# Moving the q pooling, the transposes and the last norms to other places in a kernel's fixed instruction order

## Chip, cores, metric

One core of a Trainium2 chip. The metric is the device time of one execution in microseconds (us), median of several runs. A profile of one execution has a span 1.7 to 2.3 us shorter than the time of the same run; where I compare stretches I use profiles, where I compare kernels I use timed runs. All runs here were in the fast state. Engines: PE (TensorE matmul), PEld (its weight loads), DVE (VectorE), ACT (ScalarE), POOL (GpSimd, which from slot 1 on only issues transfers).

## The reference

Attention on q averaged over pairs of positions (8 batches, 8 heads, 1152 positions, 64 wide), then a gated linear unit whose gate is a causal convolution of five taps over positions.

```python
q_pool = q.reshape(B, H, S // 2, 2, D).mean(axis=3)
scores = scale * np.matmul(q_pool, k.transpose(0, 1, 3, 2))
attn = softmax(scores)                       # over the last axis
x = np.matmul(attn, v)                       # then heads side by side: (B, S/2, 512)
gate_pre[:, s] = sum over k of conv_w[k] * x[:, s - 4 + k]
out = (sigmoid(gate_pre) * (x @ w_val)) @ w_out
```

The kernel uses that the scores are small: it replaces the softmax by its first order, so each head needs only sums and a Gram matrix of k and v, and it checks a bound on the norms at the end (the "norms" and "stat" below feed that check; an exact path exists and is not taken).

## The kernel before

The instruction order of every engine is fixed by the order in the program. (Slot 8 in the trace: while the transposes waited for 0.73 us, the value tile behind them did not start.) Sixteen slots handle two pairs of heads each, a = 2m and b = 2m + 1. Even and odd slots interleave different pieces of the second layer. These are the pieces that matter:

```python
def pool_q(n):                       # DVE: average over position pairs, as a sum
    qv = loaded.pop(n).rearrange("p h (u e d) -> p h u e d", u=U, e=2)
    nc.vector.tensor_tensor(out=qpv, in0=qv[:, :, :, 0, :], in1=qv[:, :, :, 1, :], op=ALU.add)

def transposes(n):                   # PE: 6 transposes of the pooled q; ACT copies them to SBUF
    qt_ps = ps_t.tile([128, Sq], BF16, name="qt_ps", tag="ts")      # one buffer, shared with "sm"
    ...

def sums(n): ...                     # PE: 18 matmuls into "sm" (buffer "ts")
def grams(n): ...                    # PE: 18 matmuls into g
def rows(m): ...                     # DVE: needs sm; rank1(m) on PE needs rows
def norms(m, g): ...                 # PE: 10 tiny matmuls over the squares of slot m
def stat(m, g): ...                  # DVE: copies norms out; ACT's xevac needs it
def squares(m, g): ...               # ACT
def xhat(n, at): ...                 # PE into PSUM buffer b<at>;  xevac(n): ACT
def conv(n, at): ...                 # PE into b<at>: two of the five taps
def tap(n, i): ...                   # DVE: the other three; tap 0 reads conv's PSUM
def gate(n): ...                     # ACT: sigmoid of what the taps have summed
def val(b, ft, at): ...              # PE, 8 matmuls into b<at>
def gval(b, ft, vps): ...            # DVE: gate * val, reads that PSUM buffer
def outs(...): ...                   # PE, 4 matmuls per column c into PSUM
def warm(m, at=0): ...               # PE: m matmuls on idle data, whose result nobody reads
```

The slots, cut to the lines that move (`pb` is pair b of the slot before, `moe` is true from slot 2 on):

```python
            # ---- even slot, after sums, grams, taps of pb, rank1, mevac ----
            gate(pb)
            gval(bt, 2, val(bt, 2, 0))
            norms(m - 1, g)
            stat(m, g)
            xhat(a, 1)
            xhat(b, 2)
            xevac(a)
            xevac(b)
            pool_q(a + 2)
            transposes(a + 2)
            if moe:
                v3 = val(bt, 3, 0)
                pool_q(b + 2)
                gval(bt, 3, v3)
            squares(m, g)
            conv(a, 1)
            conv(b, 2)
            tap(a, 0)
            ...                          # (slot 0 pools b + 2 here)
            tap(a, 1)
            tap(a, 2)
            outs(y, 512 * e, 2, ops, [0])
            transposes(b + 2)
            tap(b, 0)
            outs(y, 512 * e, 2, ops, [1])
            ...
            # ---- odd slot ----
            ...                          # outs, norms, stat, xhat, xevac
            pool_q(a + 2)
            outs(...)
            conv(a, 1)
            conv(b, 2)
            tap(a, 0)
            transposes(a + 2)
            pool_q(b + 2)
            gate(pb)
            tap(a, 1)
            tap(a, 2)
            gval(bt, 0, val(bt, 0, 0))
            transposes(b + 2)
            gate(a)
            gval(bt, 1, val(bt, 1, 1))
            tap(b, 0)
            squares(m, g)
            ...
    # ---- after the last slot ----
    norms(NSLOT - 1, g, start=True)
    gval(bt, 2, val(bt, 2, 0))
    gval(bt, 3, val(bt, 3, 2))
    stat(NSLOT, g)
```

All loads are issued by POOL in the order q, k, v of pair after pair, up to seven pairs ahead.

Of the kernel before, what the change touches and what calls it, by code (L numbers as in the profile page):

```python
# [54 lines left out]
def first_order(ctx, tc, q, k, v, moe_w_val, moe_conv_w, moe_w_out, out, flag):  # L55
# [9 lines left out]
    NSLOT = NPAIR // 2  # L65
# [23 lines left out]
    def big(name, i):  # L89
        return ps_b.tile([128, 2, 512], FP32, name=name, tag=f"b{i}")  # L90
# [98 lines left out]
    def pool_q(n):  # L189
        qp = work.tile([QP, U, 2, D], BF16, name="qp", tag="qp", bufs=3)  # L190
        qpv = qp.rearrange("p u h d -> p h u d")
        if n == 0:
            for h in range(2):
                qv = q0[h].rearrange("p (u e d) -> p u e d", u=U, e=2)
                nc.vector.tensor_tensor(out=qpv[:, h], in0=qv[:, :, 0, :], in1=qv[:, :, 1, :], op=ALU.add)
        else:
            qv = loaded.pop(n).rearrange("p h (u e d) -> p h u e d", u=U, e=2)
            nc.vector.tensor_tensor(out=qpv, in0=qv[:, :, :, 0, :], in1=qv[:, :, :, 1, :], op=ALU.add)  # L198
        qps[n] = qp

    def transposes(n, at=None):
        m, i = divmod(n, 2)
        qp = qps.pop(n)
        qt_ps = (ps_t if at is None else ps_b).tile([128, Sq], BF16, name="qt_ps", tag="ts" if at is None else f"b{at}")
        qtv = qt_ps.rearrange("c (u p) -> c u p", u=U)
        for u in range(U):
            nc.tensor.transpose(out=qtv[:, u, :], in_=qp[:, u].rearrange("p h d -> p (h d)"),  # L207
                                identity=ident[0:QP, 0:QP])
        nc.scalar.copy(out=mq2[m % 2][:, i, 2 * D:].rearrange("c (p u) -> c p u", u=U),  # L209
                       in_=qt_ps.rearrange("c (u p) -> c p u", u=U))  # L210
# [38 lines left out]
    def norms(m, g, start=False):  # L249
        sq = sqs.pop(m)  # L250
        for i in range(2):
            for j in range(5):
                c = 258 + 10 * i + 2 * j
                nc.tensor.matmul(out=g[:, c:c + 2], lhsT=sq[:, i, 128 * j:128 * j + 128], rhs=halves_bf,  # L254
                                 start=start and i == 0 and j == 0, stop=True, skip_group_check=True)

    def stat(m, g):
        a, z = (0 if m < NSLOT else 2), (22 if m else 2)
        nc.vector.tensor_copy(out=stats[:, m, a:z], in_=g[:, 256 + a:256 + z])  # L259
# [7 lines left out]
    def squares(m, g):  # L267
        sq = work.tile([128, 2, D + Sq], BF16, name="sq", tag="sq")
        nc.scalar.activation(out=sq[:, :, 0:D], in_=g[:, 0:256].rearrange("p (i c) -> p i c", i=2)[:, :, D:2 * D],
                             func=AF.Square, scale=C0)  # L270
        nc.scalar.activation(out=sq[:, :, D:], in_=mq2[m % 2][:, :, 2 * D:], func=AF.Square)  # L271
        sqs[m] = sq
# [62 lines left out]
    def val(b, ft, at):  # L335
        vps = big("vps", at)
        for fi in range(NFT):
            x = xs[(b * NP + fi) % NX]
            for half in range(2):
                c0 = PAD + half * HALF  # L340
                nc.tensor.matmul(out=vps[:, half, 0:HALF], lhsT=wval_sb[:, fi, ft * 128:(ft + 1) * 128],  # L341
                                 rhs=x[:, c0:c0 + HALF], start=(fi == 0), stop=(fi == NFT - 1))
        return vps

    def gval(b, ft, vps):
        y, e = divmod(b, 2)
        if e == 0:
            gvs[y, ft] = gate_pool.tile([128, 2 * Sq], BF16, name="gv", tag=f"gv{ft}", bufs=1)
        nc.vector.tensor_tensor(out=gvs[y, ft][:, e * Sq:(e + 1) * Sq].rearrange("p (c n) -> p c n", c=2),  # L349
                                in0=vps[:, :, 0:HALF],  # L350
                                in1=gates.pop(b * NP + ft).rearrange("p (c n) -> p c n", c=2), op=ALU.mult)
# [59 lines left out]
    def warm(m, at=0):  # L411
        wps = big("wps", at)
        for _ in range(m):
            nc.tensor.matmul(out=wps[:, 0, :], lhsT=idle[:, 0:128], rhs=idle, start=True, stop=True,  # L414
                             skip_group_check=True)
# [13 lines left out]
    for m in range(NSLOT):  # L429
        a, b = 2 * m, 2 * m + 1  # L430
        pb = b - 2
        odd = m % 2
        if m == 0:
            sums(a)
            grams(a)
            transposes(b, 1)
            setup_conv()
            sums(b)
            rows(m)
            grams(b)  # L440
        else:
            sums(a)
            sums(b)
            rows(m)
            grams(a)
            grams(b)
            tap(pb, 1)
            tap(pb, 2)
        rank1(m)
        g = gs.pop(m)  # L450
        mevac(m, g)
        if not odd:

            bt = m // 2 - 1
            y, e = divmod(bt, 2)
            moe = bt >= 0
# [3 lines that stand above are left out]
            else:  # L460
                warm(3)
            if m:
# [4 lines that stand above are left out]
            xevac(a)  # L467
            xevac(b)
            pool_q(a + 2)
            transposes(a + 2)  # L470
            if moe:
                v3 = val(bt, 3, 0)
                pool_q(b + 2)
                gval(bt, 3, v3)
            else:
                warm(3)
            squares(m, g)
            conv(a, 1)
            conv(b, 2)
            tap(a, 0)  # L480
            if not moe:
                pool_q(b + 2)
            tap(a, 1)
            tap(a, 2)
            if moe:
                ops = big("ops", 0)
                outs(y, 512 * e, 2, ops, [0])
            else:
                warm(2)
# [4 lines that stand above are left out]
                oevac(y, 512 * e, 2, ops)  # L494
            else:
                warm(2)
            gate(a)
        else:

            bt = (m - 1) // 2  # L500
            y, e = divmod(bt - 1, 2)
            moe = bt > 0
            if moe:
                if e:
                    ops = big("ops", 0)
                    outs(y, 1024, 1, ops)
                    oevac(y, 1024, 1, ops)
                else:
                    ops = big("ops", 0)
                    outs(y, 256, 2, ops, [0])  # L510
            else:
                warm(3)
# [5 lines that stand above are left out]
            xevac(b)  # L518
            if m + 1 < NSLOT:
                pool_q(a + 2)  # L520
            if moe:
                if e:
                    ops = big("ops", 0)
                outs(y, 256 + 512 * e, 2, ops, [0, 1] if e else [1])
                oevac(y, 256 + 512 * e, 2, ops)
            else:
                warm(3)
            conv(a, 1)
            conv(b, 2, full=m + 1 == NSLOT)
            tap(a, 0)  # L530
            if m + 1 < NSLOT:
                transposes(a + 2)
                if m > 1:
                    pool_q(b + 2)
            gate(pb)
            tap(a, 1)
            tap(a, 2)
            if m + 1 == NSLOT:
                gate(b)
            gval(bt, 0, val(bt, 0, 0))  # L540
            if 1 < m < NSLOT - 1:
# [3 lines that stand above are left out]
            if m + 1 < NSLOT:  # L545
                tap(b, 0)
            squares(m, g)
            if m == 1:
                warm(12)
                pool_q(b + 2)  # L550
                transposes(b + 2)
        while nload < min(NPAIR, a + NKV + 1):
            load_pair(nload)
            nload += 1
        if nload == NPAIR:
            while held:
                store(*held.pop(0), nc.gpsimd)


    g = ps_g.tile([128, 512], FP32, name="g", tag="g")  # L560
    norms(NSLOT - 1, g, start=True)
    gval(bt, 2, val(bt, 2, 0))
    gval(bt, 3, val(bt, 3, 2))
    stat(NSLOT, g)
    bound_reduce()
    y, e = divmod(bt, 2)
# [166 lines left out]
```

## Time and profile before

| | before |
|---|---|
| timed, median of 3 runs | 184.79 us (183.93 to 185.87) |
| span of the profile | 182.4 us |
| PE / DVE / ACT busy | 158.2 / 126.0 / 110.9 us |
| even slot 8, 10 (start to start) | 9.51, 9.74 us |
| odd slot 9, 11 | 9.38, 8.65 us |
| PE idle before the first transposes of an even slot, 2 to 14 | 0.73 us |

How to read the views: a line of the page or of the groups gives an engine's busy time; the timeline gives start and length of each stretch of like instructions, and in brackets how long the engine stood idle before and what ended it; the chain of waits is followed back from the last instruction. PE's reported ends are modelled (in slot 8 a value tile is reported as 1.15 us, and the next group starts 0.99 us after the tile's start), so I take the distance from one start to the next start for PE. (The windows in the prediction are cut at 119.50 and 128.20, where the sums of slots 11 and 12 begin at 119.52 and 128.17; hence its 9.72 and 8.70 for what is 9.74 and 8.65 from start to start.) The lines on which the reading rests are in the prediction below.

### The profile page before, as it was taken

Reading aid. Unit: us, or ns where it says so; the run is one execution under the profiler, and the core shown is the slowest. Engines: PE = TensorE matmul, PEld = TensorE weight load, DVE = VectorE, ACT = ScalarE, POOL = GpSimd, SP = SyncE. Lnnn points to the kernel's source line nnn. Section 1 sums busy time; section 2 is a strip of 40 time slices with the busy share of each in tenths; the row PEclk is TensorE's granted clock in tenths of the full one; section 3 lists DMA queues with packets and bytes.
Section 4 is the critical chain, followed back from the end, with each engine's and each line's share of the span. In section 5 each row is a group of like instructions: output and inputs, shape, how many; then the busy total and the mean of one; then the engine's idle time right before and its main releaser. Section 6 shows DMA issues by size and latency. Waiting matters only on the chain.

```text
span 182.4 us, 5370 instructions
## 1 busy us (share of the span) xinstructions
PE 158.2 (87%) x2277; PEld 111.5 (61%) x2277; DVE 126.0 (69%) x236; ACT 110.9 (61%) x183; POOL 77.3 (42%) x122
## 2 busy tenths in 40 slices
PE   7558898889998999899989999899989998997910
PEld 2146475566776667667776777577857676765400
DVE  3315678378699767978797859786978597955540
ACT  2122865347696777675967685868676878574120
POOL 7954414554544444444545444453543334410000
PEclk9957999999999999999999999999999999999985
DMA  5999999999999999999999999999999999994070
GB/s 191 275 208 210 204 206 207 207 207 207 207 206 208 208 207 207 208 206 209 205 207 208 206 207 207 206 207 207 207 207 207 222 383 414 417 390 199 0 282 20
DMA packets 27864, 40.11 MB, mean 220 GB/s; under 512 B 1909, under 2 KB 24757, under 8 KB 27834
## 3 DMA queue, kind: packets, MB, share of 16 engines
q0 software_dynamic: 26624, 36.61, 101.5%
q1 hardware_dynamic: 938, 2.50, 4.0%
q10 hardware_dynamic: 272, 0.59, 0.9%
q8 instruction: 20, 0.33, 0.7%
q14 instruction: 10, 0.08, 0.1%
HBM read 58.73 MB, written 9.44 MB: 374 GB/s over the span
## 4 chain that ended last, share of the span: by engine, by line
PE 57%; DVE 20%; DMA 13%; issue 4%; ACT 1%; POOL 1%; DVEq 0%; POOLq 0%
PE ops L357 18%; DMA qn<-in_q_dram 13%; PE vps L341 10%; DVE acc L318 6%; PE cps L303 6%; PE sm L219 6%; DVE acc L313 5%; PE g L229 5%; PE xh L280 4%; DVE qp L198 3%; PE qt_ps L207 3%; DVE gv L349 3%; PE g L254 2%; PE g L243 2%; PE wps L414 2%
## 5 line engine op out<-in xcount | busy, mean ns | idle before, releaser
L318 DVE SCALAR_TENSOR_TENSOR acc<-x,convw_sb,acc 128x576 f32<-128x576 bf16 x62 | 50.6, 815 | 1.4
L341 PE MATMUL vps<-x,wval_sb 128*128 128x288 bf16 x256 | 36.4, 286 | 0.0
L357 PE MATMUL ops<-wout_sb,gv 128*128 128x512 bf16 x144 | 36.0, 379 | 0.0
L313 DVE SCALAR_TENSOR_TENSOR acc<-x,convw_sb,cps 128x576 f32<-128x576 bf16 x31 | 25.1, 808 | 13.7 <-PE cps L303 13.7
L100 POOL DMA_DIRECT2D kv<-in_k_dram x31 | 22.2, 717 | 27.6 <-DMA kv<-in_v_dram 10.9
L99 POOL DMA_DIRECT2D qn<-in_q_dram x31 | 20.0, 645 | 29.6 <-DMA kv<-in_k_dram 11.4
L209 ACT COPY mq<-qt_ps 128x576 bf16<-128x576 bf16 x32 | 20.5, 639 | 19.7 <-PE qt_ps L207 19.0
L349 DVE TENSOR_TENSOR gv<-vps,gate 128x576 bf16<-128x576 f32 x32 | 23.5, 754 | 9.9 <-ACT mq L209 7.2
L341 PEld LDWEIGHTS <-wval_sb 128*128 128x128 bf16 x256 | 23.3, 97 | 5.8
L102 POOL DMA_DIRECT2D kv<-in_v_dram x31 | 22.2, 715 | 10.1 <-DMA qn<-in_q_dram 8.1
L287 ACT ACTIVATE x<-xh,stats 128x576 bf16<-128x576 f32 x32 | 22.0, 737 | 7.1 <-DVE stats L259 6.5
L325 ACT ACTIVATE gate<-acc 128x576 bf16<-128x576 f32 x31 | 21.3, 686 | 6.7 <-DVE acc L318 6.5
L219 PE MATMUL sm<-kv,first 128*64 128x128 bf16 x576 | 20.3, 226 | 4.7 <-ACT kv L425 3.6
L219 PEld LDWEIGHTS <-first 128*64 128x64 bf16 x576 | 17.7, 113 | 9.6 <-issue 7.7
L357 PEld LDWEIGHTS <-gv 128*128 128x128 bf16 x144 | 13.0, 97 | 11.9
L229 PE MATMUL g<-kv 128*64 128x128 bf16 x576 | 20.0, 225 | 0.0
L207 PE MATMUL qt_ps<-ident,qp 96*128 96x96 bf16 x192 | 13.8, 208 | 6.4 <-DVE qp L198 5.1
L198 DVE TENSOR_TENSOR qp<-qn 96x768 bf16<-96x768 bf16 x31 | 16.5, 547 | 3.9 <-DMA qn<-in_q_dram 3.9
L303 PE MATMUL cps<-x,diag 128*128 128x288 bf16 x128 | 18.9, 285 | 0.0
L207 PEld LDWEIGHTS <-qp 96*128 96x128 bf16 x192 | 10.9, 98 | 12.9 <-DVE qp L198 8.8
L370 ACT COPY osb<-ops 128x1024 f32<-128x1024 f32 (+1 forms) x17 | 15.9, 938 | 4.6 <-PE ops L357 4.6
L271 ACT ACTIVATE sq<-mq 128x1152 bf16<-128x1152 bf16 x16 | 18.7, 1167 | 0.0
(68 smaller groups left out, 143.3 us busy)
## 6 DMA issues: line engine op xcount, KB each, us to landing
qn<-in_q_dram POOLq DMA_DIRECT2D x31, 288.0 KB, 11.0
kv<-in_k_dram POOLq DMA_DIRECT2D x31, 288.0 KB, 10.9
kv<-in_v_dram POOLq DMA_DIRECT2D x31, 288.0 KB, 11.5
out_dram<-osb POOLq DMA_DIRECT2D x14, 512.0 KB, 9.1
out_dram<-osb SPq DMA_DIRECT2D x2, 512.0 KB, 2.9
out_dram<-osb POOLq DMA_DIRECT2D x3, 256.0 KB, 8.7
q<-in_q_dram SPq DMA_DIRECT2D x2, 288.0 KB, 4.2
k<-in_k_dram ACTq DMA_DIRECT2D x1, 576.0 KB, 4.7
```

The source lines that it names most:

```text
L100: nc.gpsimd.dma_start(out=t[:, W:2 * W].rearrange("p (h x) -> p h x", h=2), in_=k[b, h0:h0 + 2].rearrange("h (p t) d -> p h (t d)", p=128))
L102: nc.gpsimd.dma_start(out=t[:, 0:W].rearrange("p (h x) -> p h x", h=2), in_=v[b, h0:h0 + 2].rearrange("h (p t) d -> p h (t d)", p=128))
L207: nc.tensor.transpose(out=qtv[:, u, :], in_=qp[:, u].rearrange("p h d -> p (h d)"), identity=ident[0:QP, 0:QP])
L219: nc.tensor.matmul(out=sms[m][64 * h:64 * h + 64, i], lhsT=first, rhs=kvv[:, :, h, t, :], start=(i == 0 and t == 0), stop=(t == NT - 1), s ...
L229: nc.tensor.matmul(out=gs[m][64 * h:64 * h + 64, 128 * i:128 * i + 128].rearrange("p (c d) -> p c d", c=2), lhsT=kvv[:, 1, h, t, :], rhs=k ...
L287: nc.scalar.activation(out=x[:, PAD:].rearrange("p (c n) -> p c n", c=2), in_=xhs.pop(n)[:, :, 0:HALF], func=AF.Identity, bias=stats[:, m, ...
L303: nc.tensor.matmul(out=cps[:, half, 0:HALF], lhsT=w, rhs=x[:, c0:c0 + HALF], start=(i == 0), stop=(i == len(mats) - 1))
L313: nc.vector.scalar_tensor_tensor(out=acc.rearrange("p (c n) -> p c n", c=2), in0=x[:, kk:kk + Sq].rearrange("p (c n) -> p c n", c=2), scal ...
L318: nc.vector.scalar_tensor_tensor(out=accs[n], in0=x[:, kk:kk + Sq], scalar=convw_sb[:, ft, kk:kk + 1], in1=accs[n], op0=ALU.mult, op1=ALU.add)
L341: nc.tensor.matmul(out=vps[:, half, 0:HALF], lhsT=wval_sb[:, fi, ft * 128:(ft + 1) * 128], rhs=x[:, c0:c0 + HALF], start=(fi == 0), stop=( ...
L349: nc.vector.tensor_tensor(out=gvs[y, ft][:, e * Sq:(e + 1) * Sq].rearrange("p (c n) -> p c n", c=2), in0=vps[:, :, 0:HALF], in1=gates.pop( ...
L357: nc.tensor.matmul(out=ops[:, c, :], lhsT=gvs[y, ft][:, t0 + c:t0 + 128 * m:m], rhs=wout_sb[:, ft, :], start=(ft == 0), stop=(ft == NFT - 1))
```

## The change

Its intent: let PE do a value tile (8 matmuls) where it waited for a pooled q, and let DVE pool both coming q tiles while it waits for the convolution in odd slots. In addition the last norms go behind the last value tiles, and slot 1 has six warm-up matmuls fewer (`warm` in the diff).

```diff
@@ even slot
             pool_q(a + 2)
-            transposes(a + 2)
             if moe:
-                v3 = val(bt, 3, 0)
-                pool_q(b + 2)
-                gval(bt, 3, v3)
+                gval(bt, 3, val(bt, 3, 0))
             else:
                 warm(3)
+            transposes(a + 2)
             squares(m, g)
             conv(a, 1)
             conv(b, 2)
             tap(a, 0)
-            if not moe:
-                pool_q(b + 2)
+            pool_q(b + 2)
             tap(a, 1)
@@ odd slot
                 pool_q(a + 2)
+                if moe:
+                    pool_q(b + 2)
...
                 transposes(a + 2)
-                if m > 1:
-                    pool_q(b + 2)
             gate(pb)
@@ slot 1
-                warm(12)
+                warm(6)
@@ after the last slot
-    norms(NSLOT - 1, g, start=True)
     gval(bt, 2, val(bt, 2, 0))
     gval(bt, 3, val(bt, 3, 2))
+    norms(NSLOT - 1, g, start=True)
```

## The prediction

> **What bounds the kernel now.** I read the page first. Its span is 182.4 us (the timed median is 184.79 us).
>
> ```profile
> PE 158.2 (87%) x2277; PEld 111.5 (61%) x2277; DVE 126.0 (69%) x236; ACT 110.9 (61%) x183; POOL 77.3 (42%) x122
> ...
> DMA  5999999999999999999999999999999999994070
> GB/s 191 275 208 210 204 206 207 207 207 207 207 206 208 208 207 207 208 206 209 205 207 208 206 207 207 206 207 207 207 207 207 222 383 414 417 390 199 0 282 20
> ```
>
> Two things look full: TensorE (PE) and the transfers. The loads read fp32 and land bf16, so 207 GB/s landed is about 414 GB/s read, the rate that the stores show alone later. Both matter below, so I then split the steady state. The loop has 16 slots of two head pairs (a, b); even and odd slots differ. Here are slots 8, 9, 10, 11, cut at the first "sm" matmul of each:
>
> ```profile
> 90.88:100.40 9.52, 8.74 (x140) 6.34 (x140) 8.30 (x14) 6.74 (x12) 4.69 (x7) 1.00 1.19 208
> 100.40:109.78 9.38, 9.38 (x145) 6.83 (x144) 6.43 (x12) 6.95 (x11) 4.13 (x6) 1.00 1.19 206
> 109.78:119.50 9.72, 8.72 (x139) 6.33 (x138) 8.50 (x15) 6.90 (x12) 4.85 (x7) 1.00 1.20 207
> 119.50:128.20 8.70, 8.70 (x141) 6.50 (x140) 6.70 (x12) 6.47 (x11) 4.12 (x6) 1.00 1.19 207
> ```
>
> After the stretch and its length come PE, PEld, DVE, ACT and POOL busy, then clock, DMA share, GB/s. Odd slots (9, 11) show PE busy all through: 9.38 of 9.38, 8.70 of 8.70. Even slots leave PE idle for 0.78 and 1.00 us. The clock is full, so only PE's idle time, or its waits hidden in an estimated end, can be won. The timeline of slot 8 names the hole:
>
> ```profile
> 94.61 0.65 PE L280 MATMUL xh<-mq 128*128 128x288 bf16 x4
> 94.62 0.76 DVE L349 TENSOR_TENSOR gv<-vps,gate 128x576 bf16<-128x576 f32 x1
> ...
> 95.30 0.17 DVE L259 COPY stats<-g 128x22 f32<-128x22 f32 x1
> ...
> 95.39 1.01 DVE L198 TENSOR_TENSOR qp<-qn 96x768 bf16<-96x768 bf16 x2
> ...
> 95.99 0.43 PE L207 MATMUL qt_ps<-ident,qp 96*128 96x96 bf16 x6 [0.73 <-DVE qp L198]
> ...
> 96.25 1.15 PE L341 MATMUL vps<-x,wval_sb 128*128 128x288 bf16 x8
> ```
>
> PE finishes "xh" at 95.26 and the next thing in its order is the transposes of pair a+2, whose input DVE is only then pooling: it runs behind gval and stat on DVE. PE stands 0.73 us, with a value tile (8 matmuls) that needs nothing from that pool just behind.
>
> In odd slots, the chain of waits leaves PE and runs on DVE from the first tap into the next slot (slot 7 into 8):
>
> ```profile
> 87.83 0.81 DVE acc L313
> 88.64 0.47 DVE qp L198
> 89.11 0.74 DVE acc L318
> ...
> 92.74 0.35 DVE rows L235
> 93.09 0.04 issue
> 93.13 0.22 PE g L243 x2
> ```
>
> The pool of pair b+2 (0.47 us) lies inside that stretch, while DVE stood idle 1.23 us before 87.83 waiting for "cps" (2.19 us in slot 5). Last, the end, same kind of view:
>
> ```profile
> 165.81 1.06 ACT sq L271
> 166.87 0.05 issue
> 166.91 0.40 PE g L254 x10
> 167.31 2.00 PE vps L341 x16
> 169.31 3.02 PE ops L357 x14
> ```
>
> PE waits 1.30 us for the last squares, with two value tiles behind that do not need them.
>
> [...] the value tile's matmuls did not pass the waiting transposes for 0.73 us. [...] I take chain starts for PE, not sums of busy time. [...]
>
> **The change, part by part.** No work is added; six start-up warm matmuls go, everything else only moves.
>
> 1. *Even slots 2 to 14 (seven): transposes behind the second value tile.* The new order is xh, vps, transposes. That value tile reuses the PSUM buffer that gval reads until 94.62+0.76 = 95.38, so it starts at about 95.43 (with the 0.05 us that DVE to PE took at 93.09), not after the transposes that began at 95.99. That is 0.56 us. The transposes then find their input and take 0.26 us as elsewhere, not 0.43: 0.17 more. Sum 0.73. Against it: pair b+2's pool now follows the first tap. gval(3) would start at about 96.52 (value tile's end 96.42 plus 0.1), end at 97.28, the tap follows (0.81), the pool (0.5) ends near 98.6; PE, now 0.73 earlier, reaches those transposes at 98.6. I take off 0.08 for such touches: 0.65 x 7 = **4.55 us**.
>
> 2. *Odd slots 3 to 13 (six): both pools before the taps.* The 0.47 us leave the DVE stretch, if the q tile is there, and fill its idle time. PE gets back only what it lost at "rows": 0.27 us idle before rank1 in slot 6 (and alike in slots 10 and 14), about 0.07 in slots 4, 8, 12, where matmuls had just ended. 3 x 0.27 + 3 x 0.07 = **1.0 us**.
>
> 3. *Slot 1: warm 12 to 6.* Warm took 2.75 us for 12, but the pool of pair 5 ends at 33.06+0.55 = 33.61 whatever PE does, so the transposes go from 34.40 to about 33.65: 0.75. Then v of pair 5 lands at 35.59, and its sums would want to start at 35.3: **0.45 us** stays.
>
> 4. *The end: norms behind the values.* val(2) waits for gval(0)'s buffer: DVE started that pair of gval at 164.84, and 0.76 later is 165.60, so it starts at 165.65 in place of 167.31: 1.66. The norms (0.25 to 0.4) now come after the values and before the outputs: **1.3 us**.
>
> 5. *What q arrivals take back.* Pools in odd slots come 2 to 3 us earlier in their slot. The issue-to-landing view per transfer gives the landings. Pair 9's q, issued at 38.66 and 10.8 us under way, lands at 49.50. In slot 3 the new pool would be due at 49.32 minus the 1.1 us gained by then, so it waits and ends at 50.08; the tap, formerly at 50.54, gains 0.46 plus 0.47 = 0.93, against PE's 1.1 to 1.2. I take off **0.25 us**. Later q tiles, at 4.27 us a pair, land at 67.17 (13), 84.49 (17), 102.15 (21), 119.22 (25), 136.77 (29); adding 0.57 for wait and pool, the tap's largest gain there is 1.9, 2.8, 4.2, 5.3, 6.9 us, and by the terms above I expect 1.6, 2.5, 3.2, 4.1, 4.9 gained by then. So the loads stay just ahead. Even slots pool b+2 later than now, which relieves slot 2 (pair 7 landed at 40.94, pooled at 40.96).
>
> Sum: 4.55 + 1.0 + 0.45 + 1.3 - 0.25 = 7.05 us, say 7.1. 184.79 - 7.1 = **177.7 us**, 3.8% less.
>
> **Rivals.** (a) *Arrival takes over.* The margins in step 5 are as small as 0.3 us. For it: DMA never rests before 146 us, and one pair of loads takes 4.27 us, so 8.55 us a slot against 9.32 now: a slot can win no more than 0.77 on average. Against: I ask for only 0.65 in one slot and 0.27 in the next. If each odd pool waits and holds DVE's taps behind it, perhaps 2 us of the 7 are lost: 180. The last k and v land at 148.36 and slot 15 begins at 156.81, so the final floor is farther off. (b) *The buffer or DVE replaces the wait in even slots.* The second value tile must wait for gval(2), and the late pool of b+2 may hold the second transposes; if half of step 1 is lost, 180. Against: the sums worked out above close to 0.1 us, and DVE has over 1 us a slot idle. (c) *ACT becomes the bound:* "sm" shares a PSUM buffer with the transposes' output, so sums follow ACT's copy (0.64) closely. By my timing the copy ends at 99.6 and sums are due at 99.73. If it fails, 0.2 us a slot: 179. [...]
>
> **Range and chances.** The 80% range is 175.8 to 180.6: the low end is step 1 whole (0.56 us more), step 5 nothing (0.25 more), the 0.86 us by which the lowest timed run lies under the median, and a little over; the high end is rival a or b plus noise. Faster by over 2% means below 181.1, which needs over half of the sum: 0.92. Within 2%: 0.07. Slower: 0.01.
>
> **What would show it.** In the changed trace: in even slots, no PE idle of 0.73 before qt_ps, "vps" right behind "xh" with at most 0.2 idle; in odd slots both pools together, "acc" of the first tap starting on "cps" and not on a q transfer; no idle before rank1; norms at the end behind 16 vps matmuls; slot pairs of about 17.8 us where they take 18.6 (four slots: 37.3). Wrong would be: pools with idle time ended by qn transfers in slots 5 to 13, PE idle before the second qt_ps, or sums waiting on ACT's mq copy.

## The result, and the profile after

The changed kernel takes 179.92 us (median of 4 runs, 179.72 to 180.53), the kernel before, run beside it, 185.27 us (183.93 to 185.87). The ratio is 0.9726, with a 95% interval of 0.9663 to 0.9789. A ratio is the mean time of one kernel's fast runs over that of the other's in the same rounds, so it isn't quite the ratio of the two medians. So the kernel is 2.7% faster, where 3.8% had been forecast; the time lies within the range, near its upper end.

The page of the changed kernel, PE and the chain that ended last:

```profile
PE 155.6 (88%) x2253; PEld 110.7 (62%) x2271; DVE 126.9 (71%) x236; ACT 111.2 (63%) x183; POOL 77.4 (44%) x122
...
PE 40%; DVE 32%; DMA 17%; ACT 4%; issue 3%; SPq 0%; DVEq 0%; ACTq 0%; POOLq 0%
```

The work is the same but for the six warm matmuls; the span fell to 177.6 us. The shares of PE, DVE and the transfers in the chain were 57, 20 and 13% before: PE's fell and the other two rose. The same four slots as in the prediction (8, 9, 10, 11, cut at the first "sm" matmul), in the changed kernel; columns as there:

```profile
89.67:98.67 9.00, 8.68 (x138) 6.34 (x139) 8.07 (x14) 6.66 (x12) 3.55 (x6) 1.00 1.20 209
98.67:108.05 9.38, 9.33 (x143) 6.84 (x144) 6.86 (x12) 7.19 (x12) 4.82 (x7) 1.00 1.19 206
108.05:117.31 9.26, 8.74 (x138) 6.33 (x138) 8.26 (x14) 6.73 (x12) 4.16 (x7) 1.00 1.20 207
117.31:125.96 8.65, 8.60 (x138) 6.47 (x138) 7.09 (x12) 6.51 (x11) 4.14 (x6) 1.00 1.19 207
```

Odd slots kept their lengths. Even slot 8 went from 9.51 to 9.00, slot 10 from 9.74 to 9.26: shorter, but PE's busy time is still 0.32 and 0.52 us under the length of the slot (a few matmul records are missing, the page has 2253 beside 2271 weight loads, so busy reads a little low). The timeline of slot 8 after shows where:

```profile
93.28 0.65 PE L280 MATMUL xh<-mq 128*128 128x288 bf16 x4
93.29 0.76 DVE L349 TENSOR_TENSOR gv<-vps,gate 128x576 bf16<-128x576 f32 x1
...
94.05 0.54 DVE L198 TENSOR_TENSOR qp<-qn 96x768 bf16<-96x768 bf16 x1
94.10 1.15 PE L341 MATMUL vps<-x,wval_sb 128*128 128x288 bf16 x8 [0.18 <-DVE gv L349]
...
95.09 0.42 PE L207 MATMUL qt_ps<-ident,qp 96*128 96x96 bf16 x6
...
95.34 1.15 PE L303 MATMUL cps<-x,diag 128*128 128x288 bf16 x8
95.36 0.76 DVE L349 TENSOR_TENSOR gv<-vps,gate 128x576 bf16<-128x576 f32 x1 [0.76 <-PE vps L341]
...
96.33 1.03 PE L357 MATMUL ops<-wout_sb,gv 128*128 128x512 bf16 x3
96.84 0.55 DVE L198 TENSOR_TENSOR qp<-qn 96x768 bf16<-96x768 bf16 x1
97.31 1.66 DVE L318 SCALAR_TENSOR_TENSOR acc<-x,convw_sb,acc 128x576 f32<-128x576 bf16 x2
97.45 0.43 PE L207 MATMUL qt_ps<-ident,qp 96*128 96x96 bf16 x6
```

The hole of 0.73 us before the first transposes is gone; the value tile starts 0.18 us after "xh", as soon as gval has let go of its buffer. But the second transposes (97.45) now start on the end of the second pool (96.84 + 0.55 = 97.39), and that pool is late because it stands behind gval and the first tap. So from the start of the outputs (96.33) to these transposes it is 1.12 us, where it was 0.86 in the kernel before (98.32 to 99.18 in its slot 8). The end is as planned; chain of waits of the changed kernel:

```profile
160.17 1.98 PE vps L341 x16
162.14 0.04 issue
162.18 2.14 PE vps L341 x16
164.32 0.23 PE g L254 x10
```

Both stretches of value tiles run on without the 1.30 us wait for the squares.

### The profile page after: what moved, and what is told of

Its sections match the earlier page's. It is cut to its first block, busy times and chain, and to the rows that moved or that the text cites. A ratio compares the mean times of both kernels' runs of the same rounds, so it can differ in the third digit from the quotient of the medians.

```text
span 177.6 us, 5341 instructions
## 1 busy us (share of the span) xinstructions
PE 155.6 (88%) x2253; PEld 110.7 (62%) x2271; DVE 126.9 (71%) x236; ACT 111.2 (63%) x183; POOL 77.4 (44%) x122
## 4 chain that ended last, share of the span: by engine, by line
PE 40%; DVE 32%; DMA 17%; ACT 4%; issue 3%; SPq 0%; DVEq 0%; ACTq 0%; POOLq 0%
PE ops L357 13%; DVE acc L318 10%; DVE gv L349 9%; DVE acc L313 8%; PE vps L341 6%; DMA kv<-in_k_dram 6%; DMA qn<-in_q_dram 6%; PE sm L219 5%; DMA v<-in_v_dram 5%; PE g L229 5%; PE cps L303 3%; PE qt_ps L207 2%; PE xh L280 2%; DVE qp L198 2%; DVE rows L235 1%
## 5 line engine op out<-in xcount | busy, mean ns | idle before, releaser
L357 PE MATMUL ops<-wout_sb,gv 128*128 128x512 bf16 x129 | 35.3, 379 | 0.8
L341 PEld LDWEIGHTS <-wval_sb 128*128 128x128 bf16 x256 | 23.8, 97 | 8.7 <-issue 2.8
L265 ACT ACTIVATE mq<-g 64x128 bf16<-64x128 f32 x32 | 8.7, 271 | 16.8 <-PE g L245 16.6
L229 PEld LDWEIGHTS <-kv 128*64 128x64 bf16 x576 | 17.9, 113 | 0.0
```

The source lines that it names most:

```text
L229: nc.tensor.matmul(out=gs[m][64 * h:64 * h + 64, 128 * i:128 * i + 128].rearrange("p (c d) -> p c d", c=2), lhsT=kvv[:, 1, h, t, :], rhs=k ...
L341: nc.tensor.matmul(out=vps[:, half, 0:HALF], lhsT=wval_sb[:, fi, ft * 128:(ft + 1) * 128], rhs=x[:, c0:c0 + HALF], start=(fi == 0), stop=( ...
L357: nc.tensor.matmul(out=ops[:, c, :], lhsT=gvs[y, ft][:, t0 + c:t0 + 128 * m:m], rhs=wout_sb[:, ft, :], start=(ft == 0), stop=(ft == NFT - 1))
```

## The experiments

My theory after reading the trace (A in the texts): the reorder of even slots wins less than forecast because the late second pool takes a part back, and nothing else of size is missing. Rivals: the parts hinder one another, or arrival of q takes the gain. Unless said otherwise, each run was timed in 5 rounds beside the kernel before. "Slot m" lengths are taken from the first sums of a slot to those of the next, in the profiled run.

### Each part alone

Four kernels, each the kernel before with one hunk of the diff. First the even slots:

```diff
             pool_q(a + 2)
-            transposes(a + 2)
             if moe:
-                v3 = val(bt, 3, 0)
-                pool_q(b + 2)
-                gval(bt, 3, v3)
+                gval(bt, 3, val(bt, 3, 0))
...
+            transposes(a + 2)
...
             tap(a, 0)
-            if not moe:
-                pool_q(b + 2)
+            pool_q(b + 2)
```

> The kernel before with the even-slot reorder alone. Theory A (a new wait takes part of the gain): in each even slot the 0.73 us wait goes, but 0.18 us (second value tile on gval's buffer), 0.09 us (second transposes on the late pool) and about 0.17 us (those transposes then starting slowly) come instead, so even slots shorten by about 0.45 to 0.5 us and the whole by 3.2 to 3.5 us (1.8%). Theory B (the forecast's own term): 0.65 us a slot, 4.55 us (2.5%). Theory C (parts fight each other over arrivals): alone it wins 0.65 a slot, and only together with the odd part it falls to 0.48.

Measured: 181.99 us, ratio 0.9845 (0.982 to 0.9871), 2.9 us less. In the profile each of the seven even slots is 0.39 to 0.40 us shorter, every time, and no odd slot moved: 2.8 us. This is theory A in kind, a little below its figure, and it speaks against C: the part alone wins no more than it does in the whole (slot 8 went to 9.11 here; the further 0.11 of the whole is the odd part's, below). Forecast B, 0.65 a slot, is refuted.

The odd slots alone:

```diff
                 pool_q(a + 2)
+                if moe:
+                    pool_q(b + 2)
...
                 transposes(a + 2)
-                if m > 1:
-                    pool_q(b + 2)
```

> The kernel before with both q pools in front of the taps in odd slots, alone. Theory A: wins only PE's 0.28 us idle before rank1 in slots 6, 10, 14 and a little in 8 and 12, in all 0.5 to 1.0 us (0.3 to 0.5%), with no q wait since slots are not yet shortened, except at pair 9. Theory C (arrival-bound): DVE waits on q transfers in several odd slots and the time stays the same or gets worse.

Measured: 183.88 us, ratio 0.9956 (0.9929 to 0.9982), 0.8 us less. In the profile slots 6 and 14 are 0.34 us shorter, 4, 8 and 12 by 0.11 to 0.12, slot 10 by 0.08: together 1.1 us, the forecast's 1.0. Its spread over the slots is not the forecast's, which had 0.27 for slots 6, 10 and 14 alike: the sum hides two errors that nearly cancel. Slot 2 was 0.54 us longer in this profile, because q of pair 7 landed only at 42.15 (40.94 in the profile before) and DVE waited for it with gval behind; that place is not touched by this part, so it is scatter of the transfers.

Six warm matmuls fewer, alone:

```diff
-                warm(12)
+                warm(6)
```

> The kernel before with 6 instead of 12 warm matmuls in slot 1, alone. Forecast: 0.45 us sooner at slot 2, mostly eaten later. Rival: 0 within noise, since the sums of slot 2 wait for the landing of pair 5 and for ACT's copy behind the last transposes, as the changed kernel's trace suggests (its slot 2 began at 35.63 against 35.55). Granted clock unchanged at 0.966 either way.

Measured: 184.45 us, ratio 0.998 (0.9956 to 1.0004): not to be told from nothing, nor from the forecast's 0.45 us, which would be 0.9976. In the profile slot 2 began at 35.12, 0.43 us sooner than before (35.55), as forecast, and then took 0.58 us longer, since DVE waited for q of pair 7 (timeline of slot 2):

```profile
35.12 1.20 PE L219 MATMUL sm<-kv,first 128*64 128x128 bf16 x36 [0.73 <-ACT mq L209]
...
41.74 0.55 DVE L198 TENSOR_TENSOR qp<-qn 96x768 bf16<-96x768 bf16 x1 [1.70 <-DMA qn<-in_q_dram]
42.22 0.74 DVE L349 TENSOR_TENSOR gv<-vps,gate 128x576 bf16<-128x576 f32 x1
...
43.02 0.81 PE L357 MATMUL ops<-wout_sb,gv 128*128 128x512 bf16 x3 [0.51 <-DVE gv L349]
```

The pool waits 1.70 us for its transfer, gval stands behind it on DVE, and PE's outputs wait for gval. But that q landed at 41.72 in this profile and at 40.94 in the one before, a scatter like that of the run above. Had it landed at 40.94, the pool would have ended at about 41.5 (my estimate, with its 0.55 us), before the 41.63 at which gval could start (1.26 us after its value tile's 40.37), and nothing would have been given back here. So one profile does not show that the gain is always lost.

The norms behind the values, alone:

```diff
-    norms(NSLOT - 1, g, start=True)
     gval(bt, 2, val(bt, 2, 0))
     gval(bt, 3, val(bt, 3, 2))
+    norms(NSLOT - 1, g, start=True)
```

> The kernel before with the last norms behind the last value tiles, alone. Both theories: from the start of slot 15's sums to the end of the span 24.25 us where it was 25.6, so 1.3 us (0.7%), with nothing else moved.

Measured: 183.44 us, ratio 0.9938 (0.9916 to 0.9959), 1.1 us less. In the profile the stretch from slot 15 to the end is 24.26 us where it was 25.55: 1.29. As both theories had it.

The product of the four ratios is 0.9845 x 0.9956 x 0.998 x 0.9938 = 0.972. The whole change gave 0.9726. The parts add up, so no part took anything from another that the timed runs could show.

### The changed kernel again

> The changed kernel unaltered (one blank line more), so that the next runs have it on the same chip. Parts are additive if it gives 0.9845 x 0.9956 x 0.998 x 0.9938 = 0.972 of the kernel before. Even slots should again be 0.40 shorter and slots 6 and 14 0.74. Slot 2's start and slots 3 and 4 tell how far the loads' arrival scatters from run to run.

Measured: 179.56 us, ratio 0.9722 (0.9687 to 0.9757). Even slots from 6 on have the same lengths to 0.01 us as in the first profile. Slot 2 began at 34.88 (35.63 in the first), and slot 4 then took 9.89 (9.36): q of pair 9 landed at 50.16 and was waited for. Slot 5 began at 62.49 in this run and at 62.64 in the first. So between these two profiles the difference at the start is mostly levelled out in slots 3 and 4, since pair 9 landed at nearly the same time in both (50.31 in the first).

### The second pool early in even slots

The changed kernel, but in even slots 4 to 14 pair b + 2 is pooled before the second gval again, as in the kernel before. Transposes stay behind the value tile.

```diff
-                gval(bt, 3, val(bt, 3, 0))
+                v3 = val(bt, 3, 0)
+                if m > 2:
+                    pool_q(b + 2)
+                gval(bt, 3, v3)
...
             tap(a, 0)
-            pool_q(b + 2)
+            if m <= 2:
+                pool_q(b + 2)
```

> The changed kernel, but with pair b+2 pooled between stat and the second gval in even slots 4 to 14, as the kernel before had it, where DVE idles 0.76 us. Theory A (the late pool costs 0.25 us of each even slot, at the second transposes): the 0.09 us of PE idle and the slow outputs before it go, even slots 4 to 14 shorten by 0.25 each, 1.5 us in all (0.8%), to about 178.4. Theory B (transposes behind the outputs are slow whatever feeds them): no change. Theory C (q arrival): DVE waits for q in slots 4, 6, 8 and gval with it, so no gain or a loss.

Measured: 177.90 us, ratio 0.9641 (0.9604 to 0.9678) beside 0.9722 for the changed kernel on the same chip: 0.992 of it. In the profile slots 6, 8, 10, 12 and 14 are each 0.25 to 0.26 us shorter than in the changed kernel. Timeline of its slot 8:

```profile
93.67 1.05 DVE L198 TENSOR_TENSOR qp<-qn 96x768 bf16<-96x768 bf16 x2
93.71 1.15 PE L341 MATMUL vps<-x,wval_sb 128*128 128x288 bf16 x8 [0.18 <-DVE gv L349]
...
94.97 0.76 DVE L349 TENSOR_TENSOR gv<-vps,gate 128x576 bf16<-128x576 f32 x1 [0.25 <-PE vps L341]
...
95.94 1.03 PE L357 MATMUL ops<-wout_sb,gv 128*128 128x512 bf16 x3
...
96.81 0.42 PE L207 MATMUL qt_ps<-ident,qp 96*128 96x96 bf16 x6
```

In the changed kernel's slot 8 DVE had waited 0.76 us for the value tile; the second pool fills 0.5 of them, gval still starts 1.26 us after the tile (95.36 - 94.10 before, 94.97 - 93.71 here), and the second transposes follow the outputs after 0.87 us instead of 1.12. This undoes the loss without touching anything else on PE, so the late pool is shown to be its cause; theories B and C fall. The 0.18 us on gval's buffer stays.

### And pair 9 pooled late in slot 3

```diff
                 pool_q(a + 2)
-                if moe:
+                if m > 3:
                     pool_q(b + 2)
...
                 transposes(a + 2)
+                if m == 3:
+                    pool_q(b + 2)
```

> The same, and in odd slot 3 alone the pool of pair 9 goes back behind the first tap. Theory A with arrival costing only there: 0.28 us of PE idle before rank1 in slot 4 goes too, so about 0.3 us under the run before it, 1.8 us under the changed kernel, about 178.1. If arrival costs nothing in slot 3, it is the same as the run before it.

> The version x_best again, beside the run above on the same chip: ratio 0.9635 to the kernel before, slot 5 beginning at about 62.3, even slots from 6 on at 8.74 (9.00 in slot 10).

Measured: 177.92 us, ratio 0.9635 (0.9609 to 0.9662), and on another chip 178.16 us, ratio 0.9615 (0.9584 to 0.9646). The expected further 0.3 us are not there: slot 4 took 8.91 us, where the run without this edit had 8.74. Slot 4 began 0.40 us sooner here (53.37 against 53.77), and in it DVE reached the pool of pair 11 before its q had landed (58.91) and waited 0.51 us; there the start was given back in part, and slot 5 began at 62.28 against 62.51. In the profile of the repeat, even slots from 6 on took 8.73 to 8.75 (9.00 in slot 10), as expected, but slot 5 began at 61.53 and not at 62.3: slot 2 had begun 0.75 us sooner than in the first profile, and pairs 9 and 11 had landed 0.76 sooner as well. A gain at the start is kept, then, when the later arrivals come sooner too. The timed runs don't tell the two apart. Both are about 1% faster than the changed kernel.

### No wait for q at all

A wrong result on purpose: every pool from pair 1 on reads one resident tile, while all the loads still run.

```diff
+    qfix = consts.tile([QP, 2, 2 * U * D], BF16, name="qfix")
+    nc.vector.memset(qfix, 0.05)
...
-            qv = loaded.pop(n).rearrange("p h (u e d) -> p h u e d", u=U, e=2)
+            loaded.pop(n)
+            qv = qfix.rearrange("p h (u e d) -> p h u e d", u=U, e=2)
```

> Wrong result on purpose: the changed kernel with every pool from pair 1 on reading one resident tile, so no pool waits for a q transfer; all loads still run. If arrival of q is the main reason that 2 us of the forecast are missing: about 2 us faster than the changed kernel. By theory A it is not: only slot 1 (then held by v of pair 5 at about 36) and slot 3 gain, 0.3 to 0.9 us, and even slots 6 to 14 keep their lengths of 9.00 to 9.27.

Measured: 179.47 us, ratio 0.971 (0.9683 to 0.9736), against 0.9722 for the changed kernel on the same chip: no difference that the intervals show, and not one of 2 us. Whether slots 1 and 3 won the 0.3 to 0.9 us of theory A can't be told from them. (The comparison with the reference passed all the same, so it cannot see the part of the result that depends on q.) Even slots 6, 8, 12 and 14 keep 9.00 to 9.01. So arrival of q does not explain the missing part. Slot 10 alone fell from 9.26 to 9.01. In the changed kernel the second gval of slot 9 starts 0.92 us after the first, where it is 0.67 in slot 13, and PE then stands 0.20 us before rank1 of slot 10; here that is gone. The view puts 0.17 us of the pause down to ACT's gate, but in slot 13 that gate runs at the same place and delays nothing. The same pause stands in the run with the odd part alone, where slot 10 won only 0.08. Its cause stays open.

### Output weights loaded later

The early slots still wait for arrivals (0.51 us for q of pair 11 in slot 4 of x_best). This is the version x_best with the 512 KB of output weights issued behind pair 5 instead of ahead of pair 4.

```diff
-    nc.gpsimd.dma_start(out=wout_sb, in_=moe_w_out.rearrange("(ft p) n -> p ft n", p=128))
...
             load_pair(nload)
             nload += 1
+            if nload == 6:
+                nc.gpsimd.dma_start(out=wout_sb, in_=moe_w_out.rearrange("(ft p) n -> p ft n", p=128))
```

> The version x_best with the load of the output weights issued behind pair 5 and not ahead of pair 4. It tests whether the first slots are paced by arrival. If so: q of pair 4 lands some 2.5 us sooner (about 26), slot 2 begins 1 to 2.5 us sooner, and most of it is lost again by slot 5, because pairs 9 and 11 land when they did (v of 9 at about 53.2, v of 11 at about 61.8): slot 5 begins no sooner than about 61.5 against 62.3, and the whole wins 0.3 to 0.8 us. If arrival does not pace the start: slot 2 begins as before, at about 35.7.

Measured: 178.07 us, ratio 0.9604 (0.9577 to 0.963), beside 178.16 and 0.9615 for x_best on the same chip: no difference that the intervals show. In the profile q of pair 4 landed at 25.54 instead of 28.23, and slot 1 had no wait for it; yet slot 2 began at 36.07. In that execution the granted clock was one half for 10.24 us near the start, in that of x_best beside it for 6.83 (the mean over the run is 0.956 against 0.972), and slot 1 began at 24.42 against 22.43. So the profile does not compare like with like. The two ratios differ by 0.001, with intervals of 0.003 to each side: the forecast's 0.3 to 0.8 us is neither shown nor excluded. That stays open.

## Why the prediction came out as it did

**What bounds it: right.** PE with its waits, not the transfers, set the pace of the steady state before and after: from slot 5 on the trace of the changed kernel shows PE idle for over 0.1 us only on gval's buffer (0.18 in each even slot) and before rank1 of slot 10 (0.20); its wait for the late pool is hidden in modelled ends (it shows from start to start, 1.12 us where it was 0.86). Odd slots from 3 on, which had no such wait, kept their lengths to 0.01 us. Whether the loads could come sooner was not shown: no run changed their rate, and about 207 GB/s lands in SBUF in both profiles. So rival a's 0.77 us a slot is an estimate, from the 4.27 us of a pair.

**Step 1, even slots: right mechanism, mis-sized, and this is most of the missing part.** The forecast had 0.56 (no wait before the transposes) + 0.17 (the transposes shorter) - 0.08 (touches) = 0.65 us a slot. From start to start, slot 8 of the kernel before and of the changed kernel give the table below; the even part alone agrees to 0.01 us. Its lines for the kernel before, as far as the prediction doesn't show them:

```profile
97.24 1.15 PE L303 MATMUL cps<-x,diag 128*128 128x288 bf16 x8
...
97.51 0.76 DVE L349 TENSOR_TENSOR gv<-vps,gate 128x576 bf16<-128x576 f32 x1 [1.12 <-ACT mq L209]
...
98.32 1.02 PE L357 MATMUL ops<-wout_sb,gv 128*128 128x512 bf16 x4
...
99.18 0.42 PE L207 MATMUL qt_ps<-ident,qp 96*128 96x96 bf16 x6
```

| from start to start on PE | before | after | gain |
|---|---|---|---|
| xh to the next group (transposes; value tile after) | 1.38 | 0.82 | 0.56 |
| value tile, first transposes (0.99 + 0.26) | 1.25 | 1.24 | 0.01 |
| convolutions to outputs | 1.08 | 0.99 | 0.09 |
| first outputs to second transposes | 0.86 | 1.12 | -0.26 |
| the rest to the next sums | 1.22 | 1.22 | 0 |

The 0.56 came in full, by exactly the buffer wait that the forecast worked out (0.18 left). The 0.17 was not there: the chain gives the transposes 0.43 because it runs to their modelled end (96.42), but the timeline in the prediction has the value tile start at 96.25, and six transposes take 0.26 from start to start either way. In its place there were 0.09, since in the kernel before the outputs had waited for the second gval's buffer (97.51 + 0.76 = 98.27, outputs at 98.32). The touches were 0.26 and not 0.08. The forecast saw the risk (rival b) and worked it to a tie: pool done at 98.6, PE there at 98.6. The error was to let gval start 0.1 us behind the end of the value tile's 0.99 us of issue; DVE starts 1.26 us after the tile's first matmul. That made gval 0.17 us late; the tap took 0.08 less than assumed and the pool 0.05 more, so the pool ended some 0.13 us later than thought, counted from the value tile. PE was there 0.09 sooner, and the transposes started 0.06 after the pool's end: together the 0.26, to 0.02. So rival (b), the late pool, came true in part. Net 0.40 a slot, 2.8 us for seven, where the forecast had 4.55: 1.75 us of the difference.

**Step 2, odd slots: right in the sum, in part by luck.** 1.1 us alone in the profile against 1.0: slots 6 and 14 won more than forecast (0.34 for 0.27), slot 10 less (0.08 for 0.27), because of the pause in slot 9 that stays open. In the whole, slots 6 and 14 show it (0.74 = 0.40 + 0.34) and 8 and 12 (0.51 = 0.40 + 0.11).

**Step 3, warm-up: right for the start of slot 2, not shown to stay.** Alone, slot 2 does begin 0.43 us sooner; in that profile the arrival of pair 7 took it back, and the timed runs (0.37 us less, with an interval of -0.07 to 0.81) fit both 0 and 0.45. In the profile of the changed kernel slot 2 began 0.08 later than before, q of pair 4 having landed 0.8 us later (its pool started on it at 28.91, before at 28.11); in the second profile 0.67 sooner, and slot 4 took most of it back. 0.5 us of the difference in the first profile.

**Step 4, the end: right.** 1.3 us forecast, 1.33 in the whole, 1.29 alone.

**Step 5, arrivals: right in place, a little small.** Pair 9 is the one whose wait costs, 1.34 us on DVE in slot 3 of the changed kernel. It left slot 4 with 0.15 us of gain where the sum of the parts is 0.51: 0.36 us lost against 0.25 forecast. After that one of the signs of being wrong did show: in slot 5 the pool of pair 13 waited 0.45 us for its transfer. It cost nothing, as slot 6 still won its 0.74. In later slots no pool waited, as forecast; rival a did not come, which the run without q waits shows too.

In sum for the profile: 7.05 forecast, less 1.75 (step 1), less 0.5 (step 3), less 0.1 (step 5), plus 0.1 (step 2) is 4.8, and the span fell by 182.4 - 177.6 = 4.8 us. Rival c (ACT's copy) did not come: no idle PE before sums was put down to that copy from slot 4 on. The granted clock there is 1.00.

## What to carry to other kernels

When an engine is moved past a wait, follow the instructions that are pushed back in the other engine's order: here the second pool went behind a tap, where it gave back 0.26 of the 0.66 us won in a slot, and putting it into DVE's remaining wait brought the time to 177.9 us, 3.6% under the kernel before. Work out such near ties from starts of the consumer as the trace shows them (here 1.26 us after the first of eight matmuls, which take 0.99 us to the next start and are reported as 1.15), not from modelled ends. And near the start, ask what arrives when: in x_best slot 4 began 0.40 us sooner, DVE waited 0.51 us there for q of pair 11, and 0.23 us was left at slot 5; in its repeat that q came 0.76 us sooner, and slot 5 began 0.75 us sooner than in x_best.
